# Rounding the float64 weights in units of two pieces, with their power words kept in a spare part of the second weight

## The chip, the cores and the metric

The kernel runs on one core of a Trainium2 chip. The metric is the device time of one execution in microseconds. All times below are microseconds unless marked ns.

## What is computed

Inputs are `q`, `k`, `v` of shape (8, 8, 576, 64) and two weights, `w_ch1` (512 x 2048) and `w_ch2` (2048 x 512). The weights reach the device as 64-bit floats.

```python
attn = softmax(q_c @ k_c.T / 8)           # per chunk of 64 positions
x    = (attn @ v_c)                       # (8, 576, 512)
u    = x + real(fft(fft(x, axis=1), axis=2))
un   = (u - mean(u)) / sqrt(var(u) + 1e-6)
out  = u + relu(un @ w_ch1) @ w_ch2
```

## The kernel before, in words

The 4608 rows of x make 36 tiles of 128 rows, taken in ten groups of up to four tiles. For each group there is an MLP: an "up" product with `w_ch1`, a Relu, and a "down" product with `w_ch2`. While TensorE runs the MLP of one group, the attention and the Fourier mixing of a later batch are threaded between its steps. The order of all instructions is written out by hand: a loop (L1190 to L1224) takes one step of the MLP generator, then as many steps of the side generator (attention, Fourier) as are due, then some rounding of weights. Each engine runs its own instructions in the order in which this loop emitted them.

The first group's up product is `up_first` (L924). It has 16 steps; in each, four matmuls of 128x512 read one block of `w_ch1`. Four steps make one block of four PSUM tiles, after which ScalarE copies them out with Relu (L940) and the next block's matmuls reuse the four PSUM buffers. The down product of the first group is `down_plain` (L963), again 16 steps of four matmuls (L970), each with one block of `w_ch2`.

[...] There are 32 pieces of 128x512 elements: pieces 0 to 15 are the blocks of `w_ch1` in the order in which `up_first` needs them, 16 to 31 those of `w_ch2`. A piece comes by DMA as 512 KB of raw words (L285, issued on SyncE's queue) into one of seven spaces, which lie in `yall` and in rows of `xall` that are not yet in use. `round_weight(i)` (L287) then emits the first half of piece i and the second half of piece i - 1:

- first half: VectorE masks the high word twice, into the weight's place (L306) and into a tile `power` (L309); ScalarE turns the fraction to a float (L300) and the exponent into a power of two with two Relus (L303, L304).
- second half: VectorE adds the low word (L318), puts the sign into the power (L319) and multiplies (L320). Then the raw space is free and the load of a later piece is issued.

`round_next` (L1147) calls `round_weight` once. The loop calls it once per MLP step that has no heavy side step beside it, and twice in the first four steps and some later ones. The tile `power` comes from a pool of three tiles that also holds other intermediate results. When all rounding has been emitted and step 23 is reached, VectorE forms combinations of `w_ch2` (L897) that are written to DRAM for later groups.

The side work that touches the change: per attention tile a pair of VectorE instructions on the scores (maximum L394, subtraction L396), ScalarE's exponential (L407), copies of transposed q and k (L360, L369) or VectorE transposes (L349), and VectorE's division of the result (L451 to L453).

Of the kernel before, what the change touches and what calls it, by code (L numbers as in the profile page):

```python
# [9 lines left out]
U32 = mybir.dt.uint32  # L10
# [6 lines left out]
def kernel(  # L17
# [32 lines left out]
    nc = tc.nc  # L50
    B, H, S, D = q.shape
    DM = H * D
    DFF = w_ch1.shape[1]
# [6 lines left out]
    KD = DM // 128  # L60
    KF = DFF // 128
# [5 lines left out]
    G = 2 * NM  # L67
# [6 lines left out]
    three_p = ctx.enter_context(tc.tile_pool(name="three", bufs=3))  # L74
# [15 lines left out]
    wa = const.tile([128, KD * DFF], FP32, name="wa")  # L90
    wb = const.tile([128, KF * DM], FP32, name="wb")
    w1 = wa.rearrange("p (k f) -> p k f", k=KD)
    w2 = wb.rearrange("p (m e) -> p m e", m=KF)
# [16 lines left out]
    yall = const.tile([128, 4, 512], FP32, name="yall")  # L110
# [6 lines left out]
    for b in range(B):  # L117
# [16 lines left out]
    NR = 3 * G  # L134
    xall = const.tile([128, NR + NP, XW], FP32, name="xall")
    place = {n: i % NR for i, n in enumerate(n for n in range(NT) if tiles[n][0] != RE)}
    place.update({n: NR + i for i, n in enumerate(rests)})
    spaces = [yall.rearrange("p a b -> p (a b)")[:, i * 1024:(i + 1) * 1024] for i in range(2)] + [
        xall[:, r:r + 2, :].rearrange("p a f -> p (a f)")[:, 0:1024]
        for r in (2 * G, 2 * G + 2, NR + 1, G, G + 2)  # L140
    ]
    N_LATE, N_EARLY, N_LAST = 5, 8, 26

    def kind(n):
        return tiles[n][0]
# [93 lines left out]
    def load_dim_tables():  # L239
        nc.sync.dma_start(out=cos_d, in_=dim_tab[:, 0, :])  # L240
        nc.sync.dma_start(out=sin_d, in_=dim_tab[:, 2, :])
# [14 lines left out]
    def turn_dim_tables():  # L256
# [9 lines left out]
    pieces = [  # L266
        (w1[:, kk, f:f + 512], w_ch1[kk * 128:(kk + 1) * 128, f:f + 512])
        for f in range(0, DFF, 512)
        for kk in range(KD)
    ] + [(w2[:, m, :], w_ch2[m * 128:(m + 1) * 128, :]) for m in range(KF)]  # L270

    power = {}

    raws, free = {}, list(range(len(spaces)))

    def raw(i):
        return spaces[raws[i]].bitcast(U32).rearrange("p (f r) -> p f r", r=2)

    def load_weight(i):

        fit = [r for r in free if (i < N_EARLY or r < N_LATE) and (i < N_LAST or r > 1)]
        if i < len(pieces) and fit:
            raws[i] = fit[0]
            free.remove(fit[0])
            nc.sync.dma_start(out=raw(i).rearrange("p f r -> p (f r)"), in_=pieces[i][1].bitcast(U32))  # L285

    def round_weight(i, later=None):  # L287

        if i < len(pieces):
            w, t = pieces[i][0], raw(i)
            lo, hi, wi = t[:, :, 0], t[:, :, 1], w.bitcast(U32)
            p = power[i] = three_p.tile([128, 512], U32, tag="o", name="power")

            def fraction(w=w, wi=wi):
                nc.scalar.activation(out=w, in_=wi, func=ACTF.Copy, scale=2.0 ** -20, bias=1.0)  # L300

            def exponent(p=p):
                nc.scalar.activation(out=p, in_=p, func=ACTF.Relu, scale=-1.0, bias=top[:, 0:1])  # L303
                nc.scalar.activation(out=p, in_=p, func=ACTF.Relu, scale=-8.0, bias=top[:, 1:2])  # L304

            nc.vector.tensor_scalar(wi, hi, 0x000FFFFF, None, ALU.bitwise_and)  # L306
            if later is None:
                fraction()
            nc.vector.tensor_scalar(p, hi, 0x7FF00000, None, ALU.bitwise_and)  # L309
            if later is None:  # L310
                exponent()
            else:
                later += [fraction, exponent]
        if 0 < i <= len(pieces):
            w, t = pieces[i - 1][0], raw(i - 1)
            lo, hi = t[:, :, 0], t[:, :, 1]
            p = power.pop(i - 1)
            nc.vector.scalar_tensor_tensor(w, lo, 2.0 ** -52, w, ALU.mult, ALU.add)  # L318
            nc.vector.scalar_tensor_tensor(p, hi, 0x80000000, p, ALU.bitwise_and, ALU.bitwise_or)  # L319
            nc.vector.tensor_tensor(out=w, in0=w, in1=p.bitcast(FP32), op=ALU.mult)  # L320
            r = raws.pop(i - 1)
            if i - 1 + len(spaces) < N_EARLY or r < N_LATE:
                free.append(r)
            load_weight(max(raws, default=i - 1) + 1)

    def turn(src):

# [476 lines left out]
    def natural(n):  # L804

        return xt(n)[:, DM:0:-1] if kind(n) == HI else xt(n)[:, 0:DM]
# [109 lines left out]
    lo, hi = slice(0, 256), slice(256, 512)  # L916
# [7 lines left out]
    def up_first():  # L924

        unT = unTs.pop(0)
        h1 = one_p.tile([128, KF, G * 128], FP32, tag="big", name="h1")
        for f in range(0, KF, 4):
            ups = [ps_f.tile([128, G * 128], FP32, tag="ff", name="up") for _ in range(4)]
            for kk in range(KD):  # L930
                for m, up in enumerate(ups, f):
                    nc.tensor.matmul(  # L932
                        out=up,
                        lhsT=w1[:, kk, m * 128:(m + 1) * 128],
                        rhs=unT[:, kk],
                        start=(kk == 0),
                        stop=(kk == KD - 1),
                    )
                    if kk == KD - 1:
                        nc.scalar.activation(out=h1[:, m], in_=up, func=ACTF.Relu)  # L940
                yield h1
# [21 lines left out]
    def down_plain(g, h1):  # L963

        dns = [ps_f.tile([128, 512], FP32, tag="ff", name="dn") for _ in groups[g]]
        for m in range(KF):
            for s, dn in enumerate(dns):
                nc.tensor.matmul(  # L970
                    out=dn,
                    lhsT=h1[:, m, s * 128:(s + 1) * 128],
                    rhs=w2[:, m, :],
                    start=(m == 0),
                    stop=(m == KF - 1),
                )
                if m == KF - 1:
                    n = groups[g][s]
                    if s < G - 1:
                        o = three_p.tile([128, DM], FP32, tag="o", name="o")  # L980
                    else:
                        o = one_p.tile([128, 2 * (HM + 1)], FP32, tag="two", name="o")[:, 0:DM]
                    nc.vector.tensor_tensor(out=o, in0=dn, in1=natural(n), op=ALU.add)
                    store(n, o)
            for j in range(G):
                due = KF - (G - j + 1)
                if m == due - 2:
                    normed(g + 1, j)
                if m == due:
                    turned(g + 1, j)  # L990
                    if j >= 2 and g + 1 >= first_of[1]:
                        combined(g + 1, j - 2)
            yield
# [121 lines left out]
    with tc.manual_schedule():  # L1115
# [14 lines left out]
        load_v(4)  # L1130
        load_tables()
        load_weight(0)
        load_dim_tables()
        for i in range(1, len(spaces)):
            load_weight(i)
        n_w = 0
        idle = ps_f.tile([128, 512], FP32, tag="ff", name="idle")
        early_xp = [ps_f.tile([128, 512], FP32, tag="ff", name="early_xp") for _ in range(2)], None
# [5 lines left out]

        put_off = []

        def round_next(later=None):  # L1147
            nonlocal n_w
            if n_w <= len(pieces):
                round_weight(n_w, later)  # L1150
                n_w += 1

        keep_warm(8)
# [35 lines left out]
        t = 0  # L1189
        for g in range(NG):  # L1190
            for _ in mlp(g):
                t += 1
                heavy = False
                if cur < len(sides):
                    t0 = 2 if cur == 0 else ready_at[cur - 1]
                    t1 = ready_at[cur]
                    due = min(sizes[cur], (t - t0) * sizes[cur] // (t1 - t0))
                    while done < due:
                        heavy = next(sides[cur], None) or heavy
                        done += 1  # L1200
                    if t >= t1:
                        for _ in sides[cur]:
                            pass
                        cur, done = cur + 1, 0
                if not heavy:
                    round_next()
                    if t <= 4 or t < KF and t % 4 == 0 or t >= KF + 3:
                        round_next()

                if n_w > len(pieces) and t >= KF + 7:  # L1210
                    for _ in range(3):
                        next(conv2, None)
                if t == begin[1] - 1:
                    for _ in conv2:
                        pass
                if begin[1] <= t < begin[1] + KF // 2:
                    for _ in range(3):
                        next(conv1, None)
                if t == begin[1] + KF // 2:
                    for _ in range(NS2):  # L1220
                        fetch(2)
                if t == begin[1] + KF:
                    for _ in range(NS1):
                        fetch(1)  # L1224
# [49 lines left out]
```

## Time and profile before

| what | value |
|---|---|
| median of 8 runs | 1091.85 (1090.15 to 1094.18) |
| the profiled execution's own time | 1093.42 |
| its span in the profile | 1091.6 |
| granted TensorE clock | 1.00 |
| rounding, first mask to last multiplication | 33.8 to 156.2 |
| first matmul of `up_first`, first matmul of `down_plain` | 52.93, 121.78 |
| VectorE busy in 54 to 82, 82 to 109, 109 to 136 | 26.68 of 28, 24.20 of 27, 25.53 of 27 |
| ScalarE busy in the same stretches | 24.84, 21.78, 13.49 |

The span is what the hardware profiler saw of one execution; the time includes 1.8 around it. A line of the timeline has start, duration, engine, source line, operation and tiles; on VectorE and ScalarE the next instruction may start before the end of the one before, so the cost of an instruction in a full queue is the distance of two starts and not its duration. The trace shows each matmul of 32-bit floats as two, so that "x8" is one step of four matmuls.

### The profile page before, as it was taken

The numbers are of one execution on the slowest core, as the hardware profiler recorded it, in microseconds if no ns is written. First come the engines' busy times: TensorE is split into PE (matmuls) and PEld (weight loads), VectorE is DVE, ScalarE is ACT, GpSimd is POOL, SyncE is SP. The second block draws the span as 40 slices with busy tenths as digits, with TensorE's granted clock in tenths as the row PEclk, the third lists the DMA queues.
The fourth block names the chain that finished last, engine by engine and source line by source line (L and its number), as shares of the span: only waits on it lengthen the run. The fifth ranks groups of instructions, "written<-read, shape, count | busy, mean of one in ns | idle before, by whom it ended". The sixth has DMA issues, their size and how long they took to land.

```text
span 1091.6 us, 18830 instructions
## 1 busy us (share of the span) xinstructions
PE 1072.7 (98%) x7016; PEld 849.8 (78%) x7016; DVE 577.5 (53%) x1260; ACT 298.3 (27%) x725; POOL 280.9 (26%) x403
## 2 busy tenths in 40 slices
PE   8999999999999999999999999999999999999998
PEld 6644454446888888888888888888888888888887
DVE  4798987314566355663565455735663534323411
ACT  4688553222112310322022211321133103101300
POOL 4300102444405240153114230514051401220140
PEclk9999999999999999999999999999999999999999
DMA  8767656678575636692669357764653455346232
GB/s 169 234 179 195 157 170 228 174 243 268 209 202 165 202 133 204 187 260 94 189 183 247 111 183 217 202 181 150 198 183 90 141 194 160 126 154 210 78 116 77
DMA packets 147970, 192.73 MB, mean 177 GB/s; under 512 B 66126, under 2 KB 104014, under 8 KB 140712
## 3 DMA queue, kind: packets, MB, share of 16 engines
q1 hardware_dynamic: 145620, 190.20, 58.3%
q8 instruction: 56, 0.92, 0.3%
q0 software_dynamic: 512, 0.68, 0.3%
q10 hardware_dynamic: 1748, 0.66, 0.2%
q14 instruction: 34, 0.28, 0.1%
HBM read 167.22 MB, written 24.12 MB: 175 GB/s over the span
## 4 chain that ended last, share of the span: by engine, by line
PE 88%; DVE 4%; DMA 3%; ACT 2%; SPq 2%; issue 1%; POOL 1%; DVEq 0%; ACTq 0%; POOLq 0%
PE pb L1065 20%; PE pa L1016 17%; PE pa L1065 15%; PE pb L1016 13%; PE dn L970 5%; PE up L949 4%; PE pt L330 3%; PE up L932 2%; PE more_z L649 2%; PE mix L697 2%; PE z L649 2%; PE xp L429 1%; PE sc L381 1%; DMA wa<-s 1%; DMA start<-in_k_dram 1%
## 5 line engine op out<-in xcount | busy, mean ns | idle before, releaser
L1016 PE MATMUL pa<-unT,wa 128*128 128x256 f32 x672 | 159.4, 380 | 1.7 <-DVE wa L1024 1.0
L1016 PEld LDWEIGHTS pa<-unT,wa 128*128 128x128 f32 x672 | 126.5, 190 | 19.4 <-DVE wa L1024 1.2
L922 POOL TENSOR_TENSOR h<-h 128x256 f32<-128x256 f32 x64 | 55.8, 879 | 267.9 <-PE pb L1016 150.5
L1065 PE MATMUL pa<-wb,h 128*128 128x256 f32 x512 | 115.6, 380 | 0.0
L1065 PE MATMUL pb<-wb,h 128*128 128x256 f32 x512 | 114.9, 379 | 0.0
L1016 PE MATMUL pb<-wa 128*128 128x256 f32 x448 | 106.6, 381 | 0.0
L1065 PEld LDWEIGHTS pa<-wb,h 128*128 128x128 f32 x512 | 96.1, 190 | 13.5 <-issue 0.5
L1065 PEld LDWEIGHTS pb<-wb,h 128*128 128x128 f32 x512 | 96.3, 190 | 12.6
L1016 PEld LDWEIGHTS pb<-wa 128*128 128x128 f32 x448 | 84.3, 190 | 11.5
L932 PE MATMUL up<-unT,wa 128*128 128x512 f32 x128 | 58.0, 600 | 2.0 <-ACT h L940 1.2
L970 PE MATMUL dn<-wb,h 128*128 128x512 f32 x128 | 57.4, 596 | 1.3 <-ACT h L940 1.3
L1065 PE MATMUL pb<-wb,yall 128*128 128x256 f32 x256 | 58.2, 381 | 0.0
L1022 DVE TENSOR_TENSOR wa<-pb,wa 128x256 f32<-128x256 f32 x56 | 23.6, 423 | 65.4 <-ACT wa L1021 65.4
L1065 PE MATMUL pa<-wb,yall 128*128 128x256 f32 x256 | 57.9, 380 | 0.0
L1065 PE MATMUL pb<-wb 128*128 128x256 f32 x256 | 57.7, 379 | 0.0
L949 PE MATMUL up<-unT,wa 128*128 128x512 f32 x128 | 56.8, 595 | 0.0
L1021 ACT COPY wa<-pa 128x256 f32<-128x256 f32 x56 | 20.9, 373 | 124.8 <-PE pa L1016 124.8
L1016 PE MATMUL pa<-wa 128*128 128x256 f32 x224 | 53.5, 382 | 0.0
L1016 PE MATMUL pb<-unT,wa 128*128 128x256 f32 x224 | 53.0, 379 | 0.2 <-DMA wa<-s 0.2
L714 POOL TENSOR_TENSOR xall<-y,xall 128x513 f32<-128x513 f32 x14 | 21.3, 1518 | 122.7 <-DVE y L708 122.7
L1065 PEld LDWEIGHTS pa<-wb,yall 128*128 128x128 f32 x256 | 47.7, 190 | 6.4
L1065 PEld LDWEIGHTS pb<-wb,yall 128*128 128x128 f32 x256 | 47.7, 190 | 6.3
(242 smaller groups left out, 1677.0 us busy)
## 6 DMA issues: line engine op xcount, KB each, us to landing
wb<-s SPq DMA_DIRECT2D x56, 1024.0 KB
wa<-s SPq DMA_DIRECT2D x196, 256.0 KB
xall<-in_moe_w_ch_dram SPq DMA_DIRECT2D x22, 512.0 KB
q<-in_q_dram SPq DMA_DIRECT2D x96, 112.0 KB
k<-in_k_dram SPq DMA_DIRECT2D x96, 112.0 KB
v<-in_v_dram SPq DMA_DIRECT2D x124, 64.0 KB
yall<-in_moe_w_ch_dram SPq DMA_DIRECT2D x10, 512.0 KB
s<-wb SPq DMA_DIRECT2D x20, 256.0 KB
```

The source lines that it names most:

```text
L330: nc.tensor.transpose(pt[:, j, :], src(j), ident)
L649: nc.tensor.matmul(out=out_, lhsT=lhsT[p], rhs=tk[p, i, T // 2 if T != 5 else 0, cols], start=start, stop=stop, skip_group_check=True,)
L697: nc.tensor.matmul(out=mix[:, cols], lhsT=zt[:, T], rhs=tab, start=(T == 0), stop=(T == 3), skip_group_check=True,)
L714: eng.tensor_tensor(out=x[:, 0:w], in0=y[:, 0:w], in1=x[:, 0:w], op=ALU.add)
L922: nc.gpsimd.tensor_tensor(out=h1[:, m, hi], in0=h1[:, m, lo], in1=h1[:, m, hi], op=ALU.subtract)
L932: nc.tensor.matmul(out=up, lhsT=w1[:, kk, m * 128:(m + 1) * 128], rhs=unT[:, kk], start=(kk == 0), stop=(kk == KD - 1),)
L949: nc.tensor.matmul(out=up, lhsT=w1[:, kk, m * 128:(m + 1) * 128], rhs=unT[:, kk], start=(kk == 0), stop=(kk == KD - 1),)
L970: nc.tensor.matmul(out=dn, lhsT=h1[:, m, s * 128:(s + 1) * 128], rhs=w2[:, m, :], start=(m == 0), stop=(m == KF - 1),)
L1016: nc.tensor.matmul(out=dst, lhsT=w[:, kk, r], rhs=rhs[o][:, kk], start=(o in (0, 1) and kk == 0), stop=(kk == 1), skip_group_check=True,)
L1021: nc.scalar.copy(a, dst)
L1022: nc.vector.tensor_tensor(out=b, in0=pbs[r][:, 0], in1=a, op=ALU.add)
L1065: nc.tensor.matmul(out=dst, lhsT=lhs[:, m], rhs=w[:, m], start=(o in (0, 2) and m == 0), stop=(m == HF - 1), skip_group_check=True,)
```

## The change

Pieces are grouped into 22 units: (0), (1), (2,3), (4,5), (6), then (7,8), (9,10), (11) and so on up to (22,23), (24,25), (26) in this pattern of two pairs and a single, and the last five pieces one by one. There are ten pairs and twelve singles. A pair's masks, Relus, additions and multiplications are each one instruction over 128x1024 elements. Its two loads stay two DMAs of 512 KB, both issued when the unit before in that space has had its last read of the raw words. The power words of a pair lie in the last four blocks of `w_ch2`'s place (`spare`), which its last pieces fill later; singles keep the pool's tile. `round_next` counts pieces: it emits a unit when as many calls have been made as the unit has pieces. `need` emits rounding early where a matmul would otherwise be emitted before its weight.

```diff
+    units = [((0,), both_y[:, 0:1]), ((1,), both_y[:, 1:2]), ((2, 3), third), ((4, 5), second), ((6,), single)]
+    last_in = [None] * 5
+    for i in range(7, 26, 5):
+        units += [((i, i + 1), both_y), ((i + 2, i + 3), third), ((i + 4,), single)]
...
+    spare = [w2[:, KF - 4 + 2 * i:KF - 2 + 2 * i, :] for i in range(2)]
...
+    def load_weight(u):
+        for j, i in enumerate(units[u][0]):
+            nc.sync.dma_start(out=raw(u)[:, j].rearrange("p f r -> p (f r)"), in_=pieces[i][1].bitcast(U32))
...
-            p = power[i] = three_p.tile([128, 512], U32, tag="o", name="power")
+            if n > 1:
+                p = spare[u % 2].bitcast(U32)
+            else:
+                p = three_p.tile([128, 1, 512], U32, tag="o", name="power")
...
-            load_weight(max(raws, default=i - 1) + 1)
+            for v, before in enumerate(last_in):
+                if before == u - 1:
+                    load_weight(v)
...
+                need(f + kk)
...
+            if g == 0:
+                need(KF + m)
...
         def round_next(later=None):
-            nonlocal n_w
-            if n_w <= len(pieces):
-                round_weight(n_w, later)
+            nonlocal n_w, owed
+            owed += 1
+            if n_w <= len(units) and (n_w == len(units) or owed >= len(units[n_w][0])):
+                owed -= len(units[n_w][0]) if n_w < len(units) else 0
+                round_weight(n_w, later)
                 n_w += 1
+        def need(i):
+            nonlocal n_w
+            u = next(u for u, unit in enumerate(units) if i in unit[0])
+            while n_w < u + 2:
+                round_weight(n_w)
                 n_w += 1
```

## The prediction

> **What bounds it now.** First the busy shares of the page: TensorE is busy 98% of the span, so 19 of 1091.6 us are all that anything could win there.
>
> ```profile
> PE 1072.7 (98%) x7016; PEld 849.8 (78%) x7016; DVE 577.5 (53%) x1260; ACT 298.3 (27%) x725; POOL 280.9 (26%) x403
> ```
>
> The change lies between 51 and 159 us. So next the waits of TensorE in the window 52 to 125, which say how much of it belongs to the rounding:
>
> ```profile
> PE dn L970 <- ACT h L940: 1.3, 1, 1.3
> PE up L932 <- ACT h L940: 1.2, 1, 1.2
> ```
>
> Both wait for the Relu copies (L940) that free the PSUM buffers after a block of four up steps. There are four such places. Two show a gap, at 69.62 (1.18) and 121.78 (1.34). The other two, 86.70 and 103.73, show next to none. The timeline of ScalarE around 86 tells why the copy is late, and the chain of waits in the same window tells that it still ended last:
>
> ```profile
> 83.64 0.63 ACT L407 ACTIVATE ex<-ex 128x512 f32<-128x512 f32 x1 [2.80 <-DVE ex L396]
> 84.18 0.61 ACT L300 ACTIVATE wa<-wa 128x512 f32<-128x512 uint32 x1
> 84.70 0.71 ACT L303 ACTIVATE power<-power,top 128x512 uint32<-128x512 uint32 x1
> 85.44 0.72 ACT L304 ACTIVATE power<-power,top 128x512 uint32<-128x512 uint32 x1
> 86.07 2.04 ACT L940 ACTIVATE h<-up 128x512 f32<-128x512 f32 x4
> ```
> ```profile
> 82.19 0.70 DVE mx L394
> ...
> 82.92 0.70 DVE ex L396
> ...
> 83.64 0.63 ACT ex L407
> 84.27 0.52 ACT wa L300
> ...
> 85.44 0.72 ACT power L304
> 86.16 0.49 ACT h L940
> ...
> 86.70 3.70 PE up L932 x8
> ```
>
> Read it so: scores end at 82.17, VectorE takes two instructions, ScalarE one exponential, then *one piece of rounding*, then the copy. TensorE's other work ends near 86.63, so 0.07 of slack is all there is. At 103.73 the same chain stands again, 17.03 later, also ending at TensorE.
>
> **Price of a unit.** One round on VectorE, from the timeline:
>
> ```profile
> 61.40 0.42 DVE L306 TENSOR_SCALAR wa<-xall 128x512 uint32<-128x512 uint32 x1
> 61.73 0.42 DVE L309 TENSOR_SCALAR power<-xall 128x512 uint32<-128x512 uint32 x1
> 62.06 0.68 DVE L318 SCALAR_TENSOR_TENSOR wa<-xall,wa 128x512 f32<-128x512 uint32 x1
> 62.67 0.69 DVE L319 SCALAR_TENSOR_TENSOR power<-xall,power 128x512 uint32<-128x512 uint32 x1
> 63.39 0.69 DVE L320 TENSOR_TENSOR wa<-wa,power 128x512 f32<-128x512 f32 x1
> 64.00 0.42 DVE L306 TENSOR_SCALAR wa<-yall 128x512 uint32<-128x512 uint32 x1
> ```
>
> 64.00 - 61.40 = 2.60: 0.67 for the two masks, 1.93 for the second half. No row has 128x1024, so I extend by shapes. L1022 (256 elements) means 423 ns and L320 (512) 692: 0.27 per 256, fixed 0.15. So 512 more elements add 0.54 to each of the three full-rate instructions, and 0.27 to a mask (420 ns less 0.15). A pair: masks 1.21, second half 3.54, together 4.75 against 5.20. Its bounds: no saving (5.20), or the masks at the rate of the other L826 TENSOR_SCALAR row (683 ns for 512), +0.53 each.
>
> ScalarE: a piece takes 86.07 - 84.18 = 1.89. Relu L1033 (256) means 415 ns, L1036 (512) 629: 0.43 per 512. A pair is 1.89 + 3 x 0.43 = 3.18, or 3.78 if nothing is saved. In the ten pairs VectorE saves 10 x 0.45 = 4.5 and ScalarE 10 x 0.60 = 6.0, at best.
>
> The Trainium skill, "VectorE: DVE Perf Modes", section "Rules for kernel authors", says to minimise the number of operations. By that rule alone the 4.5 of VectorE should go into TensorE's waits, and the sum would be up to -2.5, the two gaps closed. The rows above say that an operation queued ahead of the copies counts by its length, not by its share of a total; I go by the rows.
>
> **The change, place by place.** TensorE's order of instructions does not change. What stands before each copy on ScalarE does: at the first place one pair (7,8) instead of pieces 7 and 8; at the second pair (12,13) instead of piece 13; at the third pair (17,18) instead of 18; at the fourth pair (22,23) instead of 23.
>
> *First place.* Rounding in the steps starts at 50.99, as before. VectorE: masks (2,3) to 52.20, second half of 1 to 54.13, masks (4,5) to 55.34, second half (2,3) to 58.88, masks 6 to 59.55, second half (4,5) to 63.09, first mask (7,8) to 63.70; before, the mask of 8 ended at 67.05. TensorE needs piece 1 at 56.4, pieces 2 and 3 from 59.9 (52.93 + 2 x 3.5; 1.0 to spare), 4 at 68.4: no new wait. ScalarE is now behind its own copy of kT (64.46 to 64.93) and not behind VectorE: 64.93 + 3.18 = 68.11 for the first copy against 68.99. **-0.9** (with no saving: 68.71, -0.3).
>
> *Second and third.* VectorE is idle before the scores (1.13 and 0.55 in the timeline), so its savings help nothing here. The exponential ends where it did, a pair stands where a single stood: 3.18 - 1.89 = **+1.3** each (no saving: +1.9). Sum so far -0.9 + 2.6 = +1.7; TensorE resumes the fourth block at 105.4.
>
> *Fourth.* Before: VectorE busy to the end, transposes L349, then masks of 23 at 118.80, copy 121.15. Now, from the end of product xp (4.27 after the resumption, 109.7): division 1.04, masks 21 0.67, second half (19,20) 3.54, scores 1.33, both transposes 1.87, first mask 0.61 = 9.06, at 118.8; then 0.04 + 3.18 on ScalarE, and 0.63 from copy to matmul: 122.6 against 121.78. TensorE itself would be ready at 105.4 + 16.7 = 122.1, so most of its gap of 1.34 is eaten by the lateness of the third place. **-0.9**. Sum **+0.8**.
>
> With nothing saved on either engine the same walk gives 107.2 at the third, 111.5 + 1.04 + 0.67 + 3.87 + 1.33 + 1.87 + 0.67 = 121.0, + 3.78 + 0.67 = 125.4: **+3.6**. I take the value near +0.8, since shapes of 256 and 512 on the same engines give the slopes.
>
> *Loads.* A pair waits for two DMAs and a space comes free later. The only raw load whose landing a wait shows is the last: issued 147.3, masks released by it at 151.57, so 4.3. For (9,10), (12,13), (17,18), (19,20) my walk leaves 8 to 12 us from issue to use: hidden. Pair (14,15) goes out behind four loads of q and k near 78.7 and is used near 85.8; lateness there is covered, since VectorE then idles before the scores at 99.5. The tight one is (22,23): behind the sixteen loads of q and k (before, the queue was past them at 111.5) it goes out near 112 and 112.4 and is wanted at 118.2. Alone 4.3, at half rate 8.6: between 1.5 early and 2.8 late. I take zero and keep the late end.
>
> *Power words in the second weight.* They replace tiles and add no instruction. The place is filled only by pieces 28 to 31, after the last pair. Cost nothing.
>
> *The tail.* The last seven units end near 135.1 + 4.75 + 4.21 + 5 x 2.60 + 1.93 = 159.0 instead of 156.2. TensorE wants the last piece at 188.85. Behind it stand three L897 (2.1) and the two additions of the first mix (0.9): 162.0, when the third mix, at 162.9, wants that mix's PSUM buffer. Hidden by 0.9; beyond it, each microsecond shows.
>
> **Rivals.**
>
> (a) *Gain.* VectorE's 4.5 carry through: the copies come early at the first and fourth place and the second and third do not suffer, because the exponential and the pair overlap more than the rows say. For it: VectorE is busy 76 of the 82 us from 54 to 136. Against: it idles before the scores twice. With both gaps gone: -2.5, time 1089.3.
>
> (b) *Full-length pairs, slower.* ScalarE saves nothing on a pair, or little: it costs two pieces in front of the second, third and fourth copy. Between +0.8 at 3.18 and +3.6 at 3.78 the sum crosses +2.2 near a pair of 3.5: from there it decides. Price +3.6, time 1095.4. For it: L303 takes 712 ns where the plain Relu L1036 over as many elements takes 629, so my slope is from a cheaper form. Against: a fixed difference explains this as well.
>
> (c) *A late pair.* At the fourth place (22,23) lands later than 5.8 after its issue. Price up to +2.8 on top of 0.8, time up to 1095.5. For it: the loads of q and k just ahead share the DMA engines. Against: before, the masks waited for DMA only 1.2 in all from 50 on.
>
> (d) *It does not do what it says*: the two blocks of a pair lie far apart in the weight, and what is between them would be taken as touched, so that matmuls wait for later units. The first steps would then stall by a second half, +3.5, time 1095.3. The waits that the built instructions carry show none.
>
> **How the numbers follow.** The profiled execution took 1093.42 (span 1091.6 and 1.8 around), 1.6 over the median 1091.85; the walk adds 0.8 to it, 1094.2. The same difference on the median gives 1092.7, my forecast. Its own range is 1091 to 1093.9. Chances: forecast 0.60, (a) 0.14, (b) 0.15, (c) 0.08, (d) 0.03. The range takes in part of both, 1090.0 to 1095.5. A measurement of this kernel tells 0.2% (2.2 us) from no change, so below 1089.7 is faster and above 1094.0 slower: 0.14 by (a), 0.60, and 0.26 by (b) to (d).
>
> **What would show it.** Right: the matmul at 69.62 starts near 68.7, those at 86.70 and 103.73 show a gap of 1.3 or more with L940's counterpart as releaser, `down_plain` starts near 122.6; 128x1024 rows of about 1.23 on VectorE, 0.69 for its masks, 1.06 to 1.15 on ScalarE. Wrong: no gap at the second and third place, masks of (22,23) released by a DMA, ScalarE rows over 1.3, or a lead or lag at 122 that later waits (0.4 at 183.8, 0.9 at 228.8) swallow.

## The result

The change made the kernel slower. The median is 1096.01 (1094.97 to 1102.86, 11 runs) against 1091.97 for the kernel before on the same chip (1089.08 to 1094.18, 30 runs); the ratio is 1.0042, 95% interval 1.0032 to 1.0053. (This ratio is taken from the runs and is not the quotient of the two medians, which is 1.0037. Where the two differ, the text goes by the ratio and its interval.) The profiled execution of the changed kernel took 1096.67, with a span of 1094.9 and a granted clock of 1.00. The forecast of 1092.7 was 3.3 too low, and the range ended at 1095.5.

First the busy shares of the changed kernel's page, beside those the prediction shows:

```profile
PE 1072.9 (98%) x7016; PEld 849.7 (78%) x7016; DVE 573.6 (52%) x1210; ACT 292.3 (27%) x695; POOL 280.9 (26%) x403
```

Both kernels round each weight to 32 bits once, on the chip. VectorE lost 3.9 us of work and ScalarE 6.0, close to the forecast 4.5 and 6.0. TensorE's work is the same. So the change did what it says, and the time was lost in waits of TensorE. The starts of the four blocks behind copies, from TensorE's timeline (the bracket is its idle time just before, and what ended it):

```profile
53.06 10.57 PE L954 MATMUL up<-unT,wa 128*128 128x512 f32 x24 [0.68 <-ACT unT L860]
68.89 3.70 PE L954 MATMUL up<-unT,wa 128*128 128x512 f32 x8 [0.33 <-ACT h L962]
87.33 3.70 PE L954 MATMUL up<-unT,wa 128*128 128x512 f32 x8 [1.44 <-ACT h L962]
105.72 3.70 PE L954 MATMUL up<-unT,wa 128*128 128x512 f32 x8 [1.43 <-ACT h L962]
124.22 3.70 PE L994 MATMUL dn<-wb,h 128*128 128x512 f32 x8 [1.78 <-ACT h L962]
```

The same starts in the kernel before:

```profile
52.93 10.57 PE L932 MATMUL up<-unT,wa 128*128 128x512 f32 x24 [0.68 <-ACT unT L839]
69.62 3.70 PE L932 MATMUL up<-unT,wa 128*128 128x512 f32 x8 [1.18 <-ACT h L940]
86.70 3.70 PE L932 MATMUL up<-unT,wa 128*128 128x512 f32 x8
103.73 3.70 PE L932 MATMUL up<-unT,wa 128*128 128x512 f32 x8
121.78 3.70 PE L970 MATMUL dn<-wb,h 128*128 128x512 f32 x8 [1.34 <-ACT h L940]
```

Take the distances, since the first matmul of `up_first` lies between 51.84 and 53.95 in the profiles of this document. Before they were 16.69, 17.08, 17.03 and 18.05; now they are 15.83, 18.44, 18.39 and 18.50. The first place gained 0.86, the second and third lost 1.36 each, and the fourth, which should have gained 0.9, lost 0.45: +2.31 in all.

ScalarE at the second place, in the order of its queue (start, duration, line):

```profile
82.91 0.63 ACT L428 ACTIVATE ex<-ex 128x512 f32<-128x512 f32 x1 [4.96 <-DVE ex L417]
83.51 1.06 ACT L322 ACTIVATE wa<-wa 128x1024 f32<-128x1024 uint32 x1
84.48 1.14 ACT L325 ACTIVATE wb<-wb,top 128x1024 uint32<-128x1024 uint32 x1
85.65 1.15 ACT L326 ACTIVATE wb<-wb,top 128x1024 uint32<-128x1024 uint32 x1
86.70 2.04 ACT L962 ACTIVATE h<-up 128x512 f32<-128x512 f32 x4
```

One pair stands between the exponential and the copies: 86.70 - 83.51 = 3.19, where a single piece took 1.89.

The second loss comes later. VectorE's timeline (the bracket again is the idle time before) and then ScalarE and TensorE at the first mix:

```profile
119.67 0.69 DVE L328 TENSOR_SCALAR wb<-yall 128x1024 uint32<-128x1024 uint32 x1 [0.91 <-DMA yall<-in_moe_w_ch_dram]
...
132.53 0.17 DVE L472 TENSOR_SCALAR rd<-xp 128x8 f32<-128x8 f32 x1 [3.41 <-PE xp L450]
...
159.77 0.69 DVE L342 TENSOR_TENSOR wb<-wb,power 128x512 f32<-128x512 f32 x1
```
```profile
157.57 0.72 ACT L326 ACTIVATE power<-power,top 128x512 uint32<-128x512 uint32 x1
158.20 0.35 ACT L696 COPY zf<-z 128x256 f32<-128x256 f32 x1
...
160.32 0.17 ACT L706 COPY zr<-more_z 1x31 f32<-1x31 f32 x1
```
```profile
160.55 0.70 PE L718 MATMUL mix<-cx,zr 128*128 128x256 f32 x2 [0.82 <-ACT zr L706]
```

And in the kernel before, VectorE, ScalarE and TensorE:

```profile
127.73 0.43 DVE L306 TENSOR_SCALAR wb<-xall 128x512 uint32<-128x512 uint32 x1
...
155.50 0.69 DVE L320 TENSOR_TENSOR wb<-wb,power 128x512 f32<-128x512 f32 x1
```
```profile
153.94 0.35 ACT L675 COPY zf<-z 128x256 f32<-128x256 f32 x1
...
156.08 0.18 ACT L685 COPY zr<-more_z 1x31 f32<-1x31 f32 x1
```
```profile
156.92 0.60 PE L697 MATMUL mix<-cx,zr 128*128 128x256 f32 x2
```

VectorE waits 0.91 for the load of pair (22,23), and later idles 3.41 in a place where the kernel before rounds a piece (127.73 to 130.33): the next pair (24,25) is emitted only at its second call. The rounding ends at 160.46 and not at 156.2. On ScalarE the last piece stands just ahead of the copies of z that the first mix reads, in both kernels. Before, these copies began at 153.94 and TensorE did not wait for them; now they begin at 158.20, and the mix is spread by a gap. From the start of the down product to the end of that mix it is 37.24, before 35.80: another 1.44. So at the mix the changed kernel is 3.75 behind, at the products of 256 columns near 255 ("products at 255" below) 3.31. Of the 3.31, 2.31 are lost ahead of the down product and 1.00 behind its start. What the whole time has on top of that (0.7 by the medians, 0.2 to 2.5 by the interval) lies behind 255 and is not resolved here.

### The profile page after: what moved, and what is told of

Its sections match the earlier page's. It is cut to its first block, busy times and chain, and to the rows that moved or that the text cites. A ratio compares the mean times of both kernels' runs of the same rounds, so it can differ in the third digit from the quotient of the medians.

```text
span 1094.9 us, 18752 instructions
## 1 busy us (share of the span) xinstructions
PE 1072.9 (98%) x7016; PEld 849.7 (78%) x7016; DVE 573.6 (52%) x1210; ACT 292.3 (27%) x695; POOL 280.9 (26%) x403
## 4 chain that ended last, share of the span: by engine, by line
PE 89%; DVE 3%; ACT 2%; DMA 2%; SPq 1%; issue 1%; POOL 1%; DVEq 0%; ACTq 0%; POOLq 0%
PE pb L1089 20%; PE pa L1040 18%; PE pa L1089 15%; PE pb L1040 13%; PE up L971 4%; PE dn L994 3%; PE pt L351 3%; PE up L954 3%; PE mix L718 2%; PE more_z L670 2%; PE sc L402 2%; PE xp L450 2%; PE z L670 1%; PE idle L1167 1%; DMA wa<-s 1%
```

## The experiments

Theories: **A**, a block of ScalarE work queued ahead of the copies of h costs its length. **C**, the tail costs because the copies of z stand on ScalarE behind the last pieces. **G**, the tail costs because VectorE ends the rounding late, and what follows on VectorE has no slack. **B** is the rival that the wide instructions are slow themselves. **D** and **H** are rivals on the tail and on the fourth place; **E** and **F** are explained in the expectations that test them.

All of them in one table. The first three columns are distances from the first matmul of `up_first` in the profiled execution, and the last compares runs on one chip with the kernel before, as ratio and 95% interval.

| kernel | down product starts | rounding ends on VectorE | products at 255 | ratio |
|---|---|---|---|---|
| before | 68.85 | 103.26 | 201.91 | 1 |
| after | 71.16 | 107.40 | 205.22 | 1.0042 [1.0032, 1.0053] |
| copies_first | 65.51 | 101.75 | 200.21 | 0.9987 [0.9976, 0.9997] |
| before_copies_first | 65.51 | 102.06 | 199.78 | 0.9988 [0.9976, 0.9999] |
| before_copies_late | 71.22 | 105.39 | 204.03 | 1.0025 [1.0011, 1.0040] |
| width_undone | 71.82 | 108.37 | 206.43 | 1.0036 [1.0024, 1.0048] |
| before_spare | 68.85 | 103.45 | 201.86 | 0.9996 [0.9983, 1.0010] |
| z_copies_first | 71.35 | 108.96 | 206.83 | 1.0045 [1.0033, 1.0057] |
| before_copies_z_first | 65.51 | 102.49 | 200.05 | 0.9986 [0.9976, 0.9996] |
| copies_z_first | 65.51 | 103.51 | 201.56 | 1.0005 [0.9995, 1.0014] |
| before_tail_delay | 68.87 | 103.43 | 205.06 | 1.0029 [1.0019, 1.0039] |
| last_singles | 71.36 | 104.07 | 205.09 | 1.0041 [1.0025, 1.0057] |
| pair_at_first_call | 68.41 | 103.15 | 201.17 | 1.0017 [1.0006, 1.0028] |
| last_pair_at_first_call | 71.79 | 104.67 | 204.82 | 1.0028 [1.0015, 1.0041] |
| copies_first_first_call | 69.11 | 103.89 | 204.80 | 1.0014 [0.9999, 1.0028] |
| copies_first_last_singles | 65.52 | 102.51 | 200.55 | 0.9996 [0.9987, 1.0005] |

Read the last two columns together: a kernel whose products at 255 start later is slower by about as much, to within 1.4 us. The exception is `pair_at_first_call` (0.7 earlier, 1.9 slower). Behind 255 TensorE waits for 0.3 to 3.9 more in these profiles, most of it for a DMA into `wa`, VectorE's work on `wa` or a VectorE transpose. Not all of that comes from the edits: the kernel before has 3.2 of it, and `before_spare`, which runs the same instructions in the same order, 1.3. Also, the profiled runs of `before_copies_late` and `copies_first_first_call` took 4.9 and 3.1 more than their medians. So single profiles are compared here up to 255, and whole times by all runs.

The columns also tell the tail from what lies ahead of it. From the down product's start to the products at 255 it is 133.06 before and 134.06 after; from that start to the end of the rounding 34.41 and 36.24. In the eight kernels (the changed one among them) whose rounding ends 1.8 to 3.6 later against their own down product than before, the way to 255 is 1.0 to 3.0 longer. In the others it stays within 0.3, but for `before_tail_delay`, which delays VectorE behind the rounding, and for `last_singles` and `copies_first_first_call` (see there). This is what theory G says.

### Taking the pair out from in front of the copies

```diff
+        def release():
+            for do in held:
+                do()
+            held.clear()
...
                 t += 1
+                release()
...
-                    round_next()
+                    later = held if t < KF and t % 4 == 3 else None
+                    round_next(later)
```

`copies_first` is the changed kernel with this edit (`later` also goes to the second call).

> The changed kernel, with one difference: what a unit puts on ScalarE in the scores step just ahead of each of the four copies of h is issued behind these copies. Theory A (the pair in front of the copies costs what it is long): the gaps of TensorE at the start of up block 3 and 4 and of the down product (1.44, 1.43 and 1.78 in the changed kernel) shrink to under 0.3, the down product starts near 120 instead of 124.2; what the tail costs (about 1.4 at the mix) stays or grows by up to 1.5, so 2 to 4 us under the changed kernel, 1092 to 1094. Rival B (the 128x1024 instructions are slow for the products that use the weights, wherever they stand): the gaps move to the products' own waits for a weight, and the time stays within 1 us of the changed kernel.

1090.95 against 1091.52 for the kernel before on the same chip, ratio 0.9987 (quotient of the medians 0.9995); that is 5 under the changed kernel by the medians and 6 by the ratios. All four gaps are gone: from 52 to 125 TensorE waits once, 0.7, before the first up product. ScalarE's timeline at the second place shows why; the pair costs the same 3.2, behind the copies:

```profile
81.40 0.63 ACT L428 ACTIVATE ex<-ex 128x512 f32<-128x512 f32 x1 [3.77 <-DVE ex L417]
81.94 2.21 ACT L962 ACTIVATE h<-up 128x512 f32<-128x512 f32 x4
84.06 1.04 ACT L322 ACTIVATE wa<-wa 128x1024 f32<-128x1024 uint32 x1
```

The down product starts 5.65 earlier than in the changed kernel, more than theory A had said, and no product waits for a weight. Theory A holds, B falls: the wide instructions are all still there.

`before_copies_first` does the same to the kernel before, with single pieces.

> The kernel before (single pieces of 128x512), with the work of a piece on ScalarE in the scores step ahead of each of the four copies of h issued behind these copies. Theory A: the gaps of 1.18 at 69.62 and 1.34 at 121.78 go, the down product starts near 119.5, and if the tail follows, the time is 2 to 2.5 under the kernel before: 1089.5. Rival F (what is won at the copies is given back at the tail, because the rounding chain on VectorE and ScalarE ends where it ended, near 156): the gap appears at the first mix, and the time is within 0.7 of the kernel before.

1090.49 against 1091.52, ratio 0.9988. Both gaps go, the down product starts 3.34 earlier, and part is given back: the gap of 0.82 at the mix appears here too. Single pieces and pairs now stand level within the intervals, so no worth of the width itself is seen in the time here.

### Putting only the extra ScalarE time into the kernel before

```diff
+                if t in (7, 11):
+                    for j in range(2):
+                        nc.scalar.copy(w2[:, KF - 1 - j, :], power[n_w - 1].bitcast(FP32))
```

> The kernel before, with two further ScalarE copies of 128x512 (into rows of the second weight that are filled later, unused) behind the piece that stands ahead of the second and of the third block of copies of h: 1.1 to 1.2 more at each of these two places, nothing else changed. Theory A: a gap of 1.1 to 1.2 opens at up block 3 and 4 each, the down product starts 2.0 to 2.4 later than in the kernel before after a first place that stays (68.85 after the first up product becomes about 71), VectorE's rounding follows, and the time is 2 to 2.4 over the kernel before. Rival H (a delay at the two places is swallowed by the gap of 1.34 at the down product, because VectorE and not the copies set that place): the down product starts at most 1 later, and the time is within 1 of the kernel before.

1094.05 against 1091.66, ratio 1.0025. TensorE's timeline at the second, third and fourth place:

```profile
88.82 3.70 PE L932 MATMUL up<-unT,wa 128*128 128x512 f32 x8 [1.26 <-ACT h L940]
107.03 3.70 PE L932 MATMUL up<-unT,wa 128*128 128x512 f32 x8 [1.26 <-ACT h L940]
125.08 3.70 PE L970 MATMUL dn<-wb,h 128*128 128x512 f32 x8 [1.33 <-ACT h L940]
```

Two gaps of 1.26 open, and the fourth stays at 1.33, where it was 1.34 in the kernel before. So lateness at the second and third place is not swallowed at the fourth, because VectorE's work ahead of it moves along. In this kernel it does so through ScalarE: behind the late copies of h stands a piece of rounding, and VectorE waits for it (the bracket is the idle time; before, these two waits were 0.15 and 0.67):

```profile
109.97 0.69 DVE L318 SCALAR_TENSOR_TENSOR wb<-xall,wb 128x512 f32<-128x512 uint32 x1 [1.34 <-ACT wb L300]
111.34 0.69 DVE L319 SCALAR_TENSOR_TENSOR power<-xall,power 128x512 uint32<-128x512 uint32 x1 [0.68 <-ACT power L304]
```

Rival H falls. The 2.37 at the down product come out as about 2.7 in the time (interval 1.2 to 4.4), with nothing wide in the kernel.

### Taking the width away and leaving the grouping

```diff
-                nc.scalar.activation(out=w, in_=wi, func=ACTF.Copy, scale=2.0 ** -20, bias=1.0)
+                for j in range(n):
+                    nc.scalar.activation(out=w[:, j:j + 1], in_=wi[:, j:j + 1], func=ACTF.Copy, scale=2.0 ** -20, bias=1.0)
```

and so for each of the eight instructions of a unit.

> The changed kernel's units, loads and order, but every instruction on a pair is issued as two of 128x512, so that only the width is undone. Theory A (what counts at the copies is the length of the block queued in front, 3.19 as a pair and 3.78 as two singles in one block): 0.6 more at each of the second, third and fourth place, the gaps there near 2.0, and VectorE 4.5 more in all, of which part shows at the fourth: 2 to 4 over the changed kernel, 1098 to 1100. Rival B (the long instructions themselves are the loss): at or under the changed kernel, 1094 to 1096.

1095.49 against 1091.97, ratio 1.0036, level with the changed kernel within the intervals: the 2 to 4 that theory A added were wrong. The time alone is where rival B put it, but B is not what the trace shows: with the wide instructions gone the gaps grew. A's size was wrong because two half-width instructions of one kind, back to back, cost less than two single pieces. ScalarE's block ahead of the copies, from its timeline:

```profile
84.17 1.13 ACT L323 ACTIVATE wa<-wa 128x512 f32<-128x512 uint32 x2
85.21 2.55 ACT L328 ACTIVATE wb<-wb,top 128x512 uint32<-128x512 uint32 x4
87.67 2.02 ACT L970 ACTIVATE h<-up 128x512 f32<-128x512 f32 x4
```

87.67 - 84.17 = 3.50, between the pair's 3.19 and twice 1.89. The gaps at the second and third place are 1.67 each, 0.24 more than in the changed kernel. What hurts is that two pieces are *one block* in the queue; the width takes 0.3 of it back.

### The place of the power words alone

```diff
-            p = power[i] = three_p.tile([128, 512], U32, tag="o", name="power")
+            if i < 26:
+                p = power[i] = w2[:, KF - 4 + i % 4, :].bitcast(U32)
+            else:
+                p = power[i] = three_p.tile([128, 512], U32, tag="o", name="power")
```

> The kernel before, single pieces, with the power words of pieces 0 to 25 in the four rows of the second weight that are filled last, in place of tiles from a pool: this part of the change alone. The prediction's step says it costs nothing: within 0.7 of the kernel before, and the same order of starts on TensorE (69.6, 86.7, 103.7, 121.8). Rival: the words in the weight's rows add waits or slow accesses, over 1 slower, with 128x512 rows on VectorE or ScalarE that are longer than 0.42, 0.69 and 0.72.

1091.87 against 1092.61, ratio 0.9996 with an interval on both sides of 1. The four distances on TensorE are those of the kernel before to 0.01. This part costs nothing.

### The tail: copies of z ahead of the last piece

```diff
-                if not heavy:
+                if not heavy and t != KF + 6:
```

This moves piece 31 on ScalarE behind the copies of z and changes no other queue.

> The changed kernel, with one difference: the three ScalarE instructions of the last piece (31) stand behind the copies of z and no longer ahead of them; the order on every other engine is the same. Theory C (the copies of z queue on ScalarE behind the last rounds): in the changed kernel the last piece ends on ScalarE at 158.29 and piece 30 at 155.69, so the copies begin 2.5 earlier, the gap of 0.82 at the mix and the 0.6 by which the mix is spread go, and the time is 1.4 under the changed kernel: 1094.6. Rival D (the tail is late by what stands before it, or by VectorE): the gap at the mix stays, and the time is within 0.5 of the changed kernel.

1096.53 against 1091.97, ratio 1.0045: nothing won. The mix does come out as theory C said, without its gap (35.79 from the down product's start to its end, as before). But VectorE's last second half now waits for the piece on ScalarE, the rounding ends 1.6 later, and the products at 255 start 1.6 later. The chain of waits, read from the late piece on (start, duration, what; lines in between left out):

```profile
160.12 0.73 ACT power L326
...
160.87 0.70 DVE power L341
...
161.60 0.69 DVE wb L342
162.29 0.61 DVE yall L918
...
168.82 1.69 POOL xall L735
...
177.10 0.82 ACT un L845
```

From the last piece it runs over the end of the rounding, the conversion of `w_ch2`, the results of the mix and the normalised tile to TensorE. In this kernel TensorE then meets two waits of 1.1 and 1.2 for the division (L463), at 217 and 234. The gap at the mix was the first place where the lateness could be seen, but closing it wins nothing as long as the rounding ends late. Theory C as the sole cause falls; G stands. This run alone does not separate the two cleanly, since its edit also moved the end of the rounding; `before_tail_delay` and `last_pair_at_first_call` below do more.

The same edit was added to the two kernels with the copies of h first.

> The kernel before with single pieces, the copies of h ahead of a piece at the four places, and the copies of z ahead of the last piece on ScalarE. If the gap of 0.82 at the mix, which was seen with the copies of h first alone, comes from the last piece ahead of the copies of z, it goes: 1.5 less than that kernel, 1089.0, and 2.5 under the kernel before. If VectorE's last second half sets the mix, the gap stays and the time is that of the copies of h first alone, 1090.5.

1089.80 against 1091.97, ratio 0.9986. The gap goes as expected, and the time is that of the copies of h first alone (0.9988): what it won at the mix, 1.7, it lost by 255.

> The changed kernel with pairs, both orders of ScalarE changed: copies of h ahead of the pairs, copies of z ahead of the last piece. By theory A and C 1.5 under the copies of h first alone: 1089.4, and then level with the kernel before under the same two orders, so that the width itself is worth nothing either way (within 0.7). Rival (a) (the 4.5 that VectorE saves is worth something once nothing queues behind the pairs): at least 1 under the kernel before with the same two orders.

1092.48, ratio 1.0005. With pairs the edit costs 0.2%, with a rounding that ends 1.8 later than in `copies_first`. The expectation was wrong here: it put this kernel level with single pieces under the same two orders to within 0.7, and it is 2.7 slower than they are by the medians. Rival (a) of the prediction finds no support: pairs are nowhere ahead of single pieces.

### The tail: VectorE delayed behind the rounding

```diff
-            nc.vector.tensor_tensor(out=out_, in0=in0, in1=in1, op=op)
+            for _ in range(7 if i == 0 and out_ is o1 else 1):
+                nc.vector.tensor_tensor(out=out_, in0=in0, in1=in1, op=op)
```

> The kernel before, with the first subtraction of 128x512 behind the rounding on VectorE (L897) issued seven times and not once (same result each time): VectorE is 6 x 0.6 to 0.7, about 4, later behind the rounding, and nothing ahead of it changes. Theory G (what the changed kernel lost is lost through VectorE: from the end of the rounding on, mixes, conversions, stores and loads of k hang on it, and TensorE meets it again before 255): the final block of products near 255 starts 3 to 4 later, and the time is 3 to 4 over the kernel before, as much as the change cost. Theory A alone (the time was lost by the gaps ahead of the down product, and the tail has slack): under 1.

1095.82 against 1092.61, ratio 1.0029, so 3.2 (2.1 to 4.3). Up to the end of the first mix nothing moved (104.66 after the first up product, before 104.65). The seven instructions, from VectorE's timeline, and the two longest of TensorE's waits from 125 to 262 (before, 0.9 for rd was the longest):

```profile
155.74 5.05 DVE L898 TENSOR_TENSOR yall<-wb 128x512 f32<-128x512 f32 x7
```
```profile
PE sc L381 <- DVE rd L442: 1.7, 2, 0.9
PE mix L697 <- DVE y L708: 1.3, 1, 1.3
```

VectorE is 4.36 later behind the seven (155.74 to 160.82, before 156.11 to 156.83), and the products at 255 are 3.15 later. So behind the rounding VectorE has about 1.2 of slack in all. At the third mix alone (L708 frees its PSUM buffer) it has 3.0, since 4.36 open a wait of 1.30 there; the rest is lost at later places, most visibly at the division at 215 (a wait of 0.8). This is theory G alone, without a copy of h being late.

### Earlier or smaller last units

`last_singles`: pairs end with (19,20), and 22 to 31 are singles (the two expectations that name (20,21) as the last pair mean this).

```diff
-    for i in range(7, 26, 5):
+    for i in range(7, 20, 5):
...
+    units += [((i,), singles[(i - 22) % 5]) for i in range(22, 32)]
```

> The changed kernel with pairs only up to (20,21); from piece 22 on every piece is a unit, loaded on its own. Theory E (the fourth place is late by 1.6 over the forecast because pair (22,23) is landed late and is long, and the tail because of the pairs (24,25)): the down product starts near 122.3 to 123 instead of 124.2, the mix has no gap, together 2.5 to 3.5 under the changed kernel: 1092.5 to 1093.5, with the 1.3 of each of the second and third place still to be seen. Rival D (the tail is late only because of what lies ahead of it): only 1 to 2 under it.

1096.16 against 1091.52, ratio 1.0041: no gain, where theory E expected 2.5 to 3.5. The mix lost its gap, but the fourth place stayed at 1.99. A single piece waits there too, because one call more now fits in and both transposes stand ahead of the next piece:

```profile
121.41 1.08 DVE L371 STREAM_TRANSPOSE kT<-k 128x512 f32<-128x512 f32 x1
122.33 0.41 DVE L329 TENSOR_SCALAR wb<-yall 128x512 uint32<-128x512 uint32 x1
```

So at that place VectorE's queue sets the copies as much as the load does. Theory E (the length of the last pairs) falls. The run also bounds theory G. The rounding ends 3.3 earlier than in the changed kernel, but the products at 255 start only 0.1 earlier: from the down product to 255 it is 133.73, before 133.06. The extra sits at one wait for a division (rd, 1.35 at 233; before 0.94), which ends a chain over loads of k on SyncE's queue. Why that chain is longer here stays open.

`pair_at_first_call`: a pair is emitted at its first call.

```diff
-            if n_w <= len(units) and (n_w == len(units) or owed >= len(units[n_w][0])):
+            if n_w <= len(units) and (n_w == len(units) or owed > 0):
```

> The changed kernel, but a pair is issued at the first of its two calls and not at the second. Theory C (the last units come late because VectorE idles in the round in which a pair waits for its second call, and the copies of z queue on ScalarE behind them): VectorE's idle stretch of 3.4 before the division at 132.5 is filled, the last unit ends before 158 instead of 160.4, the gap at the first mix goes, worth about 1.4: 1094.5. Rival D (the tail is late only because the down product starts late): the gap at the mix stays and the time stays within 0.5 of the changed kernel. With both, a pair issued earlier can also come to stand in front of other copies of h, up to 1.3 a place, seen at the starts of the up blocks.

1093.94 against 1091.52, ratio 1.0017, 2 to 3 under the changed kernel. The gaps at the second and third place and at the mix vanish, and the fourth grows to 2.4, since VectorE waits 3.5 there for the load of (22,23). In its profile it stands level with the kernel before all the way, but not in its time. That difference of 1.9 (0.7 to 3.1) stays open.

`last_pair_at_first_call`: the same for (24,25) only.

> The changed kernel, but pair (24,25) alone is issued at the first of its two calls: VectorE works at it in the 3.4 in which it idles before the division at 132.5, and the two loads that follow it go out ahead of four loads of v. The gaps of TensorE at the copies of h (1.43, 1.44, 1.8) stay. Theory G: the rounding ends 2.5 to 4 earlier on VectorE than at 160.46, the start of the products near 255 moves by as much less what the down product's late start holds, and the time is 2 to 3 under the changed kernel, about 1093.5. Theory A alone: within 1 of the changed kernel.

1096.19 against 1092.61, ratio 1.0028. The rounding ends 2.7 earlier and the mix has no gap; the fourth place is 0.6 later, since VectorE waits 1.5 for (22,23) here. The products at 255 start 0.4 earlier. Counted from its own down product they start after 133.03, as in the kernel before (133.06) and not after 134.06 as in the changed kernel: the tail's loss of 1.0 is gone, and what is left is the late down product. The interval of the time overlaps that of the changed kernel, so the expected 2 to 3 are not shown.

`copies_first_first_call`: `copies_first` with the first-call rule.

> Pairs issued at the first of their two calls, and the copies of h ahead of them on ScalarE: both losses of the changed kernel undone. Theory G: the rounding ends 1 to 2 earlier than with the copies of h first alone (101.75 after the first up product), and the time falls as much: 1089 to 1090, under the kernel before by 2 to 3 and the best of all here. If the rounding's end is held by TensorE's products or by loads instead, it is that of the copies of h first alone, 1090.5 to 1091.5.

1093.53 against 1092.61, ratio 1.0014 and not the best. The rule moves pair (22,23) to a step whose ScalarE part is not held back, and its load is not there:

```profile
116.90 0.69 DVE L328 TENSOR_SCALAR wb<-yall 128x1024 uint32<-128x1024 uint32 x1 [4.42 <-DMA yall<-in_moe_w_ch_dram]
```
TensorE then waits 3.4 for the copies. This is what rival (c) describes, and more than it priced (2.8): everything ahead is early, the load lands when it lands, and the copies stand behind it. Against `copies_first`, whose copies wait for nothing there, it loses 3.6 at the down product. It loses more just behind: the first step of the down product takes 5.40 and not 3.70, and the granted clock is 0.60 in 121.4 to 123.0 and 0.51 in 123.0 to 125.2, with 1.00 before the wait and after.

`copies_first_last_singles`: both edits.

> The changed kernel with the copies of h first, and pairs only up to (20,21), single pieces after. Theory G: with the copies out of the way, what is left is the end of the rounding on VectorE; single pieces start earlier on loads that have landed, but cost VectorE 0.45 more a pair: the rounding ends within 1 of the copies of h first alone (101.75 after the first up product) and the time is within 1 of it, 1090 to 1092. If the last pairs themselves cost something at the tail, 1 to 2 less.

1090.99 against 1091.66, ratio 0.9996; rounding and time are within 1 of `copies_first`, as G says. But it is not faster than the kernel before.

**What beats both kernels.** The copies of h ahead of the rounding gain about 0.13% on the kernel before with single pieces (0.9988, and 0.9986 with the copies of z first), and as much with pairs in `copies_first` (0.9987). These three can't be told apart, and their intervals end at 0.9996 to 0.9999. With pairs the gain is less sure: the medians of `copies_first` differ by 0.05% only, and `copies_first_last_singles` (0.9996) and `copies_z_first` (1.0005), which have the same order of the copies of h, are level with the kernel before.

## Why the prediction was wrong

**Right in mechanism and size.** *Price of a unit*: the wide instructions follow each other as extrapolated. The masks are 0.69 long, the other three 1.22, and ScalarE's block is 3.19 for 3.18. *First place*: -0.86 for -0.9. *Second and third*: +1.36 each for +1.3, and `before_copies_late` shows the same with nothing wide in it. *Power words*: nothing. The rule of the Trainium skill that the prediction weighed ("VectorE: DVE Perf Modes", section "Rules for kernel authors", minimise the number of operations) agrees with the busy time: with 50 instructions fewer VectorE is busy 3.9 less. The rule says nothing of where a longer operation stands in a queue, and there the rows decided.

**Wrong: *Fourth* and *Loads*, 1.35 together.** The step gave -0.9, the trace +0.45. VectorE was free for (22,23) at 118.76 and not at 118.2. Of that, 0.3 is the later start of the block (105.72 for 105.4) and 0.2 the way from the product xp to the division, which the walk left out. Then VectorE waited 0.91 for the load, which *Loads* took as zero between 1.5 early and 2.8 late. The two loads went out at 112.61 and 113.03 and released the masks at 119.67, 7.0 and 6.6 later; the walk had left 6.2 and 5.8. From there the step's own terms hold: 3.18 on ScalarE, 0.64 to the matmul. In three later kernels the same masks also wait for the load (1.5 to 4.4), which lands 6.2 to 7.1 after the first issue. The lone load of 4.3 was too short a guide. It was not the only one whose landing a wait shows, either: in the kernel before, the masks at 139.79 wait 0.23 for a load issued at 136.25, which makes 3.5. And the thought that lateness at the third place eats the gap at the fourth is wrong by itself: in `before_copies_late` the gap stays at 1.33.

**Wrong: *The tail*, "Hidden by 0.9".** The step found nothing to pay here. It cost 1.44 at the mix, of which 1.00 is left at 255. Its sum of the last units was right: they take 23.98 from the first mask of (24,25) at 136.48, for a forecast 23.9 from 135.1, and start late because the down product does. The slack at the third mix was right as well: 3.0 in the kernel before (`before_tail_delay`), less the 2.8 by which the rounding was to end later, plus the 0.8 of TensorE, make about the 0.9, and in the changed kernel no mix waits for VectorE. The step stopped there. It did not look at ScalarE, where the last piece stands ahead of the copies of z: that gave the gap of 0.82 at the first mix. And it did not look at the divisions behind the mixes: `before_tail_delay` shows that in the kernel before VectorE's slack is 1.2 in all and not 3.0, and in the eight kernels counted below the table 0.2 to 1.1 of the late rounding is swallowed and the rest shows at 255. `z_copies_first` shows that clearing ScalarE does not help as long as the rounding ends late. This failure does not follow from the first. The rounding ends 36.24 after the start of the down product, and the forecast had 36.4 (159.0 less 122.6), so by these numbers the tail would have cost about as much with the fourth place as forecast.

Place by place, the forecast was -0.9 + 1.3 + 1.3 - 0.9 = +0.8, with nothing for the tail. Measured up to 255 it is -0.86 + 1.36 + 1.36 + 0.45 + 1.00 = +3.31.

**Rivals.** (a) is out: the second and third place lost 1.36 each. (b) did not occur: the pair is 3.19, under the 3.5 from which it decides. (c) occurred in part: the pair landed 6.6 after its second issue, over the 5.8 of its condition, and cost 0.9 of its 2.8. (d) shows nowhere: the first three steps of the up product run through in 10.57, as before. The time beyond the range came from two steps failing together, of which the prediction had priced one as a rival and the other as hidden.

**Where VectorE's saving went.** Of its waits from 54 to 136, those for scores grew from 1.7 to 7.4, and 5.5 for xp is new. Here, work that ended earlier on VectorE became waiting for TensorE's products and for a load.

## What to carry to other kernels

Before pieces of side work are merged, list what stands behind each piece on its queue, and price the merged block in front of it at its full length: here merging saved 6.0 on ScalarE and cost 1.36 at each of two copies, and with the rounding behind the copies, singles and pairs alike ended about 0.13% under the kernel before (0.9988 and 0.9987). And "hidden by so much" needs the same walk for each engine that feeds the spot, with the calls and loads that pace it; a test that delays that engine by a known amount is a cheap way to see the slack.

## What the runs showed of the hardware

In these traces an instruction that reads the result of the one just ahead on its engine starts about 0.11 later than one that does not. On VectorE, L320 follows L319 by 0.72, where L319 follows L318 by 0.61, at 128x512; at 128x1024 the same steps are 1.25 and 1.14. This fits what two half-width instructions of one kind in a row save: the second half of two pieces is 3.86 as two singles, 3.62 as alternating halves in `width_undone` (71.71 to 75.33 on VectorE) and 3.54 as one wide pair. So of the 0.32 that a pair saves there, 0.24 comes from the order and 0.08 from the width. In `width_undone` the three second halves start 1.20 to 1.21 apart, 0.60 an instruction, whatever the operation. On ScalarE, L304 follows L303, whose result it reads, by 0.74; the four Relus of `width_undone`, of which none reads the one just ahead, take 2.46, so 0.62 each.

Behind TensorE's wait of 3.35 in `copies_first_first_call` the granted clock was 0.51 to 0.60 for some 4 us, and a step that takes 3.70 elsewhere took 5.40. Behind the wait of 2.42 in `last_pair_at_first_call` it stayed at 1.00.
